# Attention output leaves PSUM in one copy and one addition per head, and is rounded and split once per pair

## The chip, the cores and the metric

The kernel runs on one core of a Trainium2 chip. The metric is the device time of one execution in microseconds (us). The matrix engine is TensorE (PE in the profile, PEld for its weight loads), the elementwise engines are VectorE (DVE), ScalarE (ACT) and GpSimd (POOL), and SyncE (SP) issues nearly all of the transfers (DMA). Matrix products are accumulated in PSUM, a memory of 128 partitions with banks of 512 float32 columns. All other data on the core lie in SBUF.

## The reference

Attention over 8 batches of 8 heads, 576 tokens, head size 64, with a decay and a causal mask; then a gated MLP over the 8 heads side by side (512 columns):

```python
scores = scale * np.matmul(q, k.transpose(0, 1, 3, 2))
cum = np.cumsum(np.log(np.clip(f, 0.0001, 1.0)), axis=-1)
scores = np.where(causal, -1000000000.0, scores + cum[:, :, :, None] - cum[:, :, None, :])
attn = np.exp(scores - np.max(scores, axis=-1, keepdims=True))
attn = attn / (np.sum(attn, axis=-1, keepdims=True) + 1e-09)
x = np.matmul(attn, v)                       # then heads side by side: [batch, 576, 512]
h = np.maximum(x @ w_in, 0.0)
u, v = h[..., :512], h[..., 512:]
v_n = (v - mean(v)) / np.sqrt(var(v) + 1e-06)
v_s = np.einsum('ts,bsd->btd', w_spatial, v_n) + b_spatial[None, :, None]
out = (u * v_s) @ w_out
```

## The kernel before

Heads are worked in 32 pairs, four pairs to a batch; a pair's first head lies on partitions 0 to 63, its second on 64 to 127. A float32 operand of a product is held as two parts, `hi` (x rounded to the type float32r) and `lo` (x - hi), and a product is the sum of hi*hi, hi*lo and lo*hi. In the first NF = 5 pairs the product of attention and values is done in plain float32 instead, with one weight operand; the first NQ = 1 pair also has plain float32 scores.

`attention` works one pair P at a time. It loads the values (`prep_v`: tile `vraw`, split into `vt` from pair 5 on), builds the score operands `ta` and `tb` of pair P + 1 by copies within SBUF (`prep`), transposes the attention of pair P (`transposes`, into `ET`), computes the scores of pair P + 1 (`scores`, `scores_tail`), loads and splits queries and keys of pair P + 2 (`split`: tile `raw`, rounded on ScalarE, line 210, subtracted on GpSimd, line 212), and multiplies by the values (`attend`, once for each head). `raw`, `vraw` and `vt` have one buffer each, so a load of the next `raw` waits until line 212 has read the last one, and a load of the next `vraw` until line 243 has (in the first five pairs: until the products have).

`attend` accumulates a head's 576 columns in two PSUM banks, `x0` (tokens 0 to 255) and `x1` (256 to 575). In the split pairs the weights are 128 columns wide, so that one half of the output partitions holds the products with the head's v_hi and the other half those with v_lo; the sum of the two halves is the result. For each bank, ScalarE rounds the first half into `xh` (line 373), VectorE subtracts it from the bank into `xl` (line 374), and, in the split pairs, VectorE adds the other half of the partitions to `xl` (line 376). After the pair's second head VectorE copies the last 64 columns of `xl` behind those of `xh` (line 416). `xh` and `xl` have five buffers: four are held by the batch that the MLP reads, and one by the pair in progress; they are taken before the first head's `attend`.

`moe` is the MLP of a batch. It reads `xh` and `xl` of four pairs in its first two stages, 5 and 8 accumulations with all four pairs in each, and then gives the four buffers back. Then come the spatial product and the output product.

The order in which instructions are issued is made by a planner at build time: it gets the instructions in the order in which the two generators `attention` and `moe` yield (attention runs ahead of the MLP by LEAD = 0.25 of a batch), and places each on its engine's queue by its own estimate of when operands and buffers are ready. On the chip each queue is then worked strictly in the planned order, SP's transfers too. A load of weights (`load64`, `load_rest`) in steps on VectorE, ScalarE and GpSimd runs beside the first pairs. The MLP can't begin a batch before its fourth pair is complete.

Of the kernel before, what the change touches and what calls it, by code (L numbers as in the profile page):

```python
# [8 lines left out]
F32 = mybir.dt.float32  # L9
# [10 lines left out]
NF = 5            # pairs of heads whose attention times v is in float32  # L20
NQ = 1            # pairs of heads whose scores are in float32
# [3 lines left out]
NB = 4            # full 128-token blocks; the last 64 tokens are the tail  # L25
TL = 512          # first token of the tail
DM = 512
TOFF = (0, 128, 384, 768)      # start of a block's scores in a head's score tile
HALVES = ((0, 256), (256, 320))      # (start, length) of the halves of the tokens
QK = 640 + S        # columns of a head's queries, then of its keys  # L30
EOFF = (0, 640, 1280, 1088, 576)   # start of a key chunk in a head's packed attention^T


def f32(ap):
    return ap.bitcast(F32)
# [3 lines left out]
def attn_gmlp_kernel(ctx: ExitStack, tc: tile.TileContext, qk, v, f, w_in, w_sp, b_sp, w_out, out):  # L39
    """Decayed causal attention, then a gated MLP with a spatial gate.  # L40

    A float32 operand x of a matrix product is held as two float32r parts, hi = x rounded to
    float32r and lo = x - hi, and a product is hi*hi + hi*lo + lo*hi, summed in float32.
    """
# [15 lines left out]
    ident = cst.tile([128, 128], F32, name="ident")  # L60
    make_identity(nc, ident)
    # [zeros 512 | causal 128 | zeros 224 | causal 64, for two stacked heads]
# [12 lines left out]
    # ---- decay rows of the score products: [-8 | c_hi], [-8 | c_lo], [c_hi | 8], [c_lo | 8],  # L75
    # the queries' columns as in qk, then the keys'; c = cumulated log decay; [-8 | c], [c | 8] in float32 ----
# [58 lines left out]
    def load64(src, dh, dl, raw, w, a, mark=None):  # L135
        """A block of a float64 weight, read as two 32-bit words: round to float32 and split."""
# [3 lines left out]
        # magnitude, at least 2**-127, so that what float32 can't hold becomes zero  # L140
        A.activation(af, hi.bitcast(F32), AF.Abs)
        V.tensor_scalar(out=af, in0=af, scalar1=2.0 ** -15, scalar2=None, op0=ALU.max)
        # sign, exponent and the upper 20 bits of the mantissa
        V.tensor_scalar(out=a, in0=a, scalar1=3, scalar2=0x3FFFFFF8, op0=ALU.logical_shift_left, op1=ALU.bitwise_and)
        V.scalar_tensor_tensor(out=w, in0=hi, scalar=0xC0000000, in1=a, op0=ALU.bitwise_and, op1=ALU.bitwise_or)
        # the lower 32 bits of the mantissa
# [6 lines left out]
    def load_first(ws):  # L153
        """What the first steps of the MLP need: w_in for the gate's half, the spatial weights."""
# [26 lines left out]
    def load_rest(n, w_v, dh, dl, tag, bufs):  # L181
        """An eighth of a weight, by way of tiles that the MLP doesn't use yet."""
        raw = mo.tile([128, NJ, 64, 2], U32, name="w64", tag=("gt0", "gt1", "o")[n % 3], bufs=1)
        w = mo.tile([128, NJ, 64], U32, name="w32", tag=tag, bufs=bufs)
        t = mo.tile([128, NJ, 64], U32, name="wa", tag=tag, bufs=bufs)
        c = slice(64 * n, 64 * n + 64)
        load64(w_v[:, :, c, :], dh[:, :, c], dl[:, :, c], raw, w[:], t[:])

# [13 lines left out]
    def split(P):  # L202
        """q and k of a pair of heads, one head on each half of the partitions, split."""
# [11 lines left out]
    def prep(P, h):  # L215
        """The operands of a head's scores: ta = [q_hi; q_lo | k_hi; k_hi], tb = [q_hi; decay | k_lo; decay]."""
# [29 lines left out]
    def qkt(o, P, h, q0, k0, n, first, final):  # L246
        """Scores of 128 queries against n keys."""
        k0 += 640
        ts = tab[P, h]
        for t in ts:  # L250
            r = 66 if len(ts) == 1 else 128 if t is ts[0] else 68
            mm(o, t[0:r, q0:q0 + 128], t[0:r, k0:k0 + n], first and t is ts[0], final and t is ts[-1])

    def scores(P, h):
        """Masked scores of a head, negated and scaled; row maxima; exp; row sums; normalised."""
# [94 lines left out]
    def attend(P, h, xh, xl):  # L350
        vt = vts[P]
        x0 = ps_a.tile([128, 512], F32, name="x0")
        x1 = ps_a.tile([128, 512], F32, name="x1")
# [16 lines left out]
        for ps, s0, n in ((x0, 0, 256), (x1, 256, 320)):  # L370
            hi = xh[m0:m0 + 64, s0:s0 + n]
            lo = xl[m0:m0 + 64, s0:s0 + n]
            last[P, h] = A.copy(hi, ps[m0:m0 + 64, 0:n])  # L373
            V.tensor_tensor(out=lo, in0=ps[m0:m0 + 64, 0:n], in1=f32(hi), op=ALU.subtract)  # L374
            if P >= NF:
                V.tensor_tensor(out=lo, in0=ps[l0:l0 + 64, 0:n], in1=f32(lo), op=ALU.add)
# [4 lines left out]
    def attention(b, ws=None):  # L381
        for P in range(b * PPB, (b + 1) * PPB):
            if P == 0:
# [3 lines left out]
                # products of zeros bring the tensor engine to its full clock before the first scores  # L387
                warm = ps_a.tile([128, 512], F32, name="x0")
                for _ in range(14):
                    mm(warm, zm[:, 0:128], zm[:, 0:512], True, True)  # L390
# [18 lines left out]
            xh = wk.tile([128, 640], F32R, name="xh", tag="xh", bufs=5)  # L409
            xl = wk.tile([128, S], F32R, name="xl", tag="xl", bufs=5)  # L410
            yield from attend(P, 0, xh, xl)
# [3 lines left out]
            yield from attend(P, 1, xh, xl)  # L415
# [7 lines left out]
    def acc(b):  # L423
        """A bank to accumulate in; the last batch has those of the attention too."""
# [193 lines left out]
```

## Time and profile before

| What | Value |
|---|---|
| Timed runs | 836.0, 832.36, 834.18 us; median 834.18 |
| Profiled execution, first to last instruction (span) | 827.5 us |
| Mean granted TensorE clock | 0.972 |
| TensorE busy | 791.4 us (96%) |
| VectorE busy | 608.6 us (74%) |
| ScalarE busy | 535.9 us (65%) |
| GpSimd busy | 464.7 us (56%) |
| Lines 373 / 374 / 376 / 416 | 49.6 / 57.4 / 48.8 / 16.8 us |

The profile has no time of the profiled execution other than its span; the timed runs contain what lies before and after it. Busy shares are averages over a start, in which weights are loaded and the first batch has no MLP beside it, a long middle, and an end without attention; the stretches are looked at one by one. Times within the span are counted from its first instruction.

### The profile page before, as it was taken

What the parts mean: (1) busy time and instruction counts of PE and PEld (TensorE: products, weight loads), DVE (VectorE), ACT (ScalarE), POOL (GpSimd) and SP (SyncE); (2) the same over time, 40 slices, a digit from 0 to 9 for tenths busy, and PEclk for the clock granted to TensorE, in tenths of its full rate; (3) what the DMA queues carried; (4) which work ended last, traced back from release to release, by engine and by line L of the source; (5) the groups of instructions that cost most, each with busy time, mean ns of one, the idle gap of its engine ahead of it and who ended that gap; (6) DMA issues with size and microseconds to landing.
All of it is one profiled execution on the core that took longest, in us unless ns stands there. A gap on an engine that the chain in (4) does not pass through costs nothing.

```text
span 827.5 us, 15557 instructions
## 1 busy us (share of the span) xinstructions
PE 791.4 (96%) x4968; PEld 711.3 (86%) x4968; DVE 608.6 (74%) x1830; ACT 535.9 (65%) x1383; POOL 464.7 (56%) x631
## 2 busy tenths in 40 slices
PE   7889898999999999999999999999999999999997
PEld 4667687879889998999899988898899988999896
DVE  5776998987788777787677776768776777776431
ACT  5888556765777657767677666666676657665331
POOL 5674788664585555555575555465664547543131
PEclk7799987999999999999999999999999999999999
DMA  8997747446653664556455564546535664430001
GB/s 234 209 260 194 192 134 183 106 109 164 165 137 96 141 170 118 128 111 165 129 129 139 139 137 117 130 105 157 150 78 124 165 154 117 109 77 13 27 1 64
DMA packets 49851, 109.16 MB, mean 132 GB/s; under 512 B 7405, under 2 KB 15597, under 8 KB 49706
## 3 DMA queue, kind: packets, MB, share of 16 engines
q1 hardware_dynamic: 49450, 107.64, 52.2%
q8 instruction: 40, 0.66, 0.3%
q10 hardware_dynamic: 320, 0.52, 0.2%
q14 instruction: 41, 0.34, 0.1%
HBM read 39.53 MB, written 10.68 MB: 61 GB/s over the span
## 4 chain that ended last, share of the span: by engine, by line
PE 71%; DVE 4%; DMA 1%; ACT 1%; POOL 1%; issue 1%; SPq 0%; ACTq 0%; POOLq 0%; DVEq 0%
PE ps L198 40%; PE sc L198 12%; PE x L198 9%; PE tp L325 6%; PE tp L198 2%; PE tp L338 2%; DMA out_dram<-o 1%; DVE vx L461 1%; DVE el L315 1%; POOL tt L277 1%; DVE xh L416 0%; ACT eh L314 0%; ACT o L534 0%; POOL mv L460 0%; DVE tt L264 0%
## 5 line engine op out<-in xcount | busy, mean ns | idle before, releaser
L277 POOL TENSOR_SCALAR tt<-tt,sm 128x128 f32<-128x128 f32 (+2 forms) x248 | 131.5, 548 | 110.8 <-DVE sm L270 91.0
L264 DVE CUSTOM_DVE_ANT_0 tt<-sc,zm 128x128 f32<-128x128 f32 (+3 forms) x256 | 122.5, 486 | 69.0 <-PE tp L325 44.5
L266 ACT ACTIVATE tt<-tt,nm 128x128 f32<-128x128 f32 (+3 forms) x256 | 144.1, 564 | 41.0 <-DVE nm L264 37.1
L314 ACT CAST eh<-tp 128x512 fp32r<-128x512 f32 (+1 forms) x270 | 110.8, 424 | 58.8 <-PE tp L325 42.0
L315 DVE TENSOR_TENSOR el<-tp,eh 128x512 fp32r<-128x512 f32 (+1 forms) x270 | 127.2, 484 | 14.7 <-ACT eh L314 11.1
L198 PE MATMUL sc<-ta 128*128 128x128 f32 (+1 forms) x372 | 122.8, 340 | 13.6 <-DVE nm L264 9.0
L198 PE MATMUL sc<-tb 68*128 68x128 f32 (+1 forms) x372 | 117.9, 325 | 2.2 <-DMA tb<-lo 1.7
L325 PE MATMUL tp<-ident,tt 128*128 128x128 f32 x640 | 115.4, 284 | 2.0 <-DVE el L315 1.1
L212 POOL TENSOR_TENSOR lo<-raw,hi 128x640 fp32r<-128x640 f32 (+1 forms) x62 | 92.3, 1509 | 21.1 <-ACT hi L210 20.9
L198 PE MATMUL x<-eh,vt 128*128 128x320 f32 (+4 forms) x378 | 102.5, 287 | 1.3 <-DVE eh L347 0.9
L510 POOL TENSOR_TENSOR gl<-u,gh 128x256 fp32r<-128x256 f32 (+1 forms) x64 | 51.8, 810 | 84.9 <-ACT gh L509 79.0
L198 PEld LDWEIGHTS sc<-ta 128*128 128x128 f32 x372 | 72.3, 196 | 22.3 <-DVE nm L264 15.9
L198 PE MATMUL x<-el,vt 128*128 128x256 f32 x324 | 91.2, 307 | 0.3 <-DVE el L315 0.3
L325 PEld LDWEIGHTS tp<-ident,tt 128*128 128x128 f32 x640 | 78.7, 143 | 13.5 <-POOL tt L277 2.6
L198 PEld LDWEIGHTS sc<-tb 68*128 68x128 f32 x372 | 72.3, 196 | 5.7 <-issue 2.7
L198 PE MATMUL ps<-sph,vnh 128*128 128x256 f32 (+1 forms) x240 | 73.4, 306 | 2.7 <-DVE u L506 1.6
L198 PEld LDWEIGHTS x<-eh,vt 128*128 128x128 f32 x378 | 71.4, 190 | 5.0 <-DVE eh L347 1.1
L198 PE MATMUL ps<-xh,winh 128*128 128x256 f32 (+1 forms) x232 | 71.1, 307 | 0.8 <-ACT u L484 0.6
L198 PE MATMUL ps<-sph,vnl 128*128 128x256 f32 (+1 forms) x240 | 71.6, 298 | 0.0
L198 PE MATMUL ps<-spl,vnh 128*128 128x256 f32 (+1 forms) x240 | 71.6, 298 | 0.0
L374 DVE TENSOR_TENSOR xl<-x,xh 64x256 fp32r<-64x256 f32 (+1 forms) x128 | 57.4, 452 | 18.5 <-ACT xh L373 16.1
L373 ACT CAST xh<-x 64x256 fp32r<-64x256 f32 (+1 forms) x128 | 49.6, 393 | 32.2 <-PE x L198 30.3
(192 smaller groups left out, 2128.9 us busy)
## 6 DMA issues: line engine op xcount, KB each, us to landing
raw<-in_dram SPq DMA_DIRECT2D x31, 608.0 KB
ta<-hi SPq DMA_DIRECT2D x62, 304.0 KB
vraw<-in_dram SPq DMA_DIRECT2D x32, 320.0 KB
tb<-hi SPq DMA_DIRECT2D x62, 160.0 KB
ta<-lo SPq DMA_DIRECT2D x62, 160.0 KB
tb<-lo SPq DMA_DIRECT2D x62, 144.0 KB
ta<-hi SPq DMA_DIRECT2D x62, 144.0 KB
out_dram<-o SPq DMA_DIRECT2D x32, 256.0 KB
```

Of the source, the lines that this page charges most:

```text
L198: T.matmul(o, l, r, start=st, stop=sp)
L212: G.tensor_tensor(out=lo[:, c], in0=raw[:, c], in1=f32(hi[:, c]), op=ALU.subtract)
L264: V.tensor_tensor_reduce(out=t, in0=sc[:, 0:n], in1=zm[:, 640 - n:640], scale=-0.125, scalar=3.0e38, op0=ALU.add, op1=ALU.min, accum_out=n ...
L266: last["exp", P, h, i] = A.activation(t, t, AF.Exp, bias=nm[:, i:i + 1], scale=-1.0, accum_out=sm[:, i:i + 1])
L277: G.tensor_scalar(out=t, in0=t, scalar1=sm[:, i:i + 1], scalar2=1.0, op0=ALU.mult, op1=ALU.mult)
L314: A.copy(h_ap, ps)
L315: V.tensor_tensor(out=l_ap, in0=ps, in1=f32(h_ap), op=ALU.subtract)
L325: T.transpose(out=tp[:, (i - c) * 128:(i - c + 1) * 128], in_=tt[h][:, TOFF[i] + 128 * c:TOFF[i] + 128 * c + 128], identity=ident)
L338: T.transpose(out=tp[:, j * 128:(j + 1) * 128], in_=tl[:, c * 128:(c + 1) * 128], identity=ident)
L373: last[P, h] = A.copy(hi, ps[m0:m0 + 64, 0:n])
L374: V.tensor_tensor(out=lo, in0=ps[m0:m0 + 64, 0:n], in1=f32(hi), op=ALU.subtract)
L510: G.tensor_tensor(out=gl[j][:, 0:nt], in0=g, in1=f32(gh[j][:, 0:nt]), op=ALU.subtract)
```

## The change

A head's 576 columns now lie side by side in one tile of two banks, `xp`: x0 is its columns 256 to 511 and x1 its columns 512 to 831, so that they are one row of 576 columns that crosses from the first bank to the second. ScalarE copies the row out in float32 in one instruction into a new tile `xf`; in the split pairs it copies the half with the v_lo products, and VectorE adds the other half in one instruction. After both heads, the whole pair (128 partitions) is rounded in one ScalarE instruction and subtracted on GpSimd in two (64 and 512 columns). `xh` and `xl` are taken only then. `xf` has no memory of its own: it takes its turn in the one buffer of `raw` (pairs 0 to 4) or of `vraw` (from pair 5). The rest of the diff removes comments.

```diff
-    def attend(P, h, xh, xl):
+    def attend(P, h, xf):
         vt = vts[P]
-        x0 = ps_a.tile([128, 512], F32, name="x0")
-        x1 = ps_a.tile([128, 512], F32, name="x1")
+        xp = ps_a.tile([128, 1024], F32, name="xp")
+        x0, x1 = xp[:, 256:512], xp[:, 512:832]
...
         m0, l0 = (0, 64) if h == 0 else (64, 0)
-        for ps, s0, n in ((x0, 0, 256), (x1, 256, 320)):
-            hi = xh[m0:m0 + 64, s0:s0 + n]
-            lo = xl[m0:m0 + 64, s0:s0 + n]
-            last[P, h] = A.copy(hi, ps[m0:m0 + 64, 0:n])
-            V.tensor_tensor(out=lo, in0=ps[m0:m0 + 64, 0:n], in1=f32(hi), op=ALU.subtract)
-            if P >= NF:
-                V.tensor_tensor(out=lo, in0=ps[l0:l0 + 64, 0:n], in1=f32(lo), op=ALU.add)
+        o = xf[m0:m0 + 64, :]
+        if P >= NF:
+            A.copy(o, xp[l0:l0 + 64, 256:832])
+            last[P, h] = V.tensor_tensor(out=o, in0=xp[m0:m0 + 64, 256:832], in1=o, op=ALU.add)
+        else:
+            last[P, h] = A.copy(o, xp[m0:m0 + 64, 256:832])
...
-            xh = wk.tile([128, 640], F32R, name="xh", tag="xh", bufs=5)
-            xl = wk.tile([128, S], F32R, name="xl", tag="xl", bufs=5)
-            yield from attend(P, 0, xh, xl)
+            xf = wk.tile([128, S], F32, name="xf", tag="raw" if P < NF else "vraw")
+            yield from attend(P, 0, xf)
             yield from transposes(P, 1)
             if nxt:
                 yield from scores(P + 1, 1)
-            yield from attend(P, 1, xh, xl)
+            yield from attend(P, 1, xf)
+            xh = wk.tile([128, 640], F32R, name="xh", tag="xh", bufs=5)
+            xl = wk.tile([128, S], F32R, name="xl", tag="xl", bufs=5)
+            A.copy(xh[:, 0:S], xf)
+            for t in (slice(TL, S), slice(0, TL)):
+                G.tensor_tensor(out=xl[:, t], in0=xf[:, t], in1=f32(xh[:, t]), op=ALU.subtract)
             V.tensor_copy(xh[:, S:640], f32(xl[:, TL:S]))
```

More of the change, by code (lines that the diff above doesn't have):

```diff
@@ L386, in attention @@
                     prep(0, h)
-                warm = ps_a.tile([128, 512], F32, name="x0")
+                warm = ps_a.tile([128, 1024], F32, name="xp")
                 for _ in range(14):
-                    mm(warm, zm[:, 0:128], zm[:, 0:512], True, True)
+                    mm(warm[:, 0:512], zm[:, 0:128], zm[:, 0:512], True, True)
                 split_rows(ws, r0s[0])
```

## Prediction

> **What bounds the kernel now.** I read the engine totals first, then stretches of the span, then who TensorE waits for.
>
> ```profile
> PE 791.4 (96%) x4968; PEld 711.3 (86%) x4968; DVE 608.6 (74%) x1830; ACT 535.9 (65%) x1383; POOL 464.7 (56%) x631
> ```
>
> The stretches (columns: PE, PEld, DVE, ACT, POOL busy us, granted clock, DMA share):
>
> ```profile
> 60.00:100.00 40.00, 37.48 (x194) 29.02 (x192) 29.52 (x97) 31.52 (x83) 24.15 (x31) 0.98 0.78 199
> 100.00:180.00 80.00, 70.07 (x402) 61.32 (x403) 76.03 (x206) 48.86 (x134) 57.95 (x78) 0.87 0.55 139
> 500.00:600.00 100.00, 96.59 (x629) 89.05 (x628) 75.92 (x232) 66.30 (x172) 56.99 (x81) 1.00 0.52 128
> ```
>
> From 200 us on TensorE is the bound: even in this stretch, the one of that part with the most idle time, it is busy for 96.6 of 100 us, at the full granted clock. Only from 100 to 180 us is another engine fuller: VectorE 76.0 of 80 us, while TensorE idles 10 us and its clock falls to 0.87. What TensorE waits for, from 100 to 200 us:
>
> ```profile
> PE sc L198 <- DVE nm L264: 6.7, 7, 1.9
> ```
>
> and from 200 to 800 us:
>
> ```profile
> PE ps L198 <- DVE u L506: 2.6, 4, 1.1
> PE sc L198 <- DVE nm L264: 2.1, 3, 1.2
> ```
>
> The longest waits of TensorE are on VectorE in both parts, but they are small: about 7 us early and 5 us in the 600 us after. The change leaves every matrix product as it is, so a lighter VectorE can give back these waits, at most the 10 us of idle time of the full stretch, and no more.
>
> **The instructions.** Groups by line and shape (busy us, mean ns):
>
> ```profile
> L373 ACT CAST xh<-x 64x320 fp32r<-64x320 f32 x64 | 26.8, 419 | 23.8 <-PE x L198 23.1
> L373 ACT CAST xh<-x 64x256 fp32r<-64x256 f32 x64 | 23.5, 366 | 8.4 <-PE x L198 7.2
> L374 DVE TENSOR_TENSOR xl<-x,xh 64x320 fp32r<-64x320 f32 x64 | 31.0, 485 | 8.8 <-ACT xh L373 7.7
> L374 DVE TENSOR_TENSOR xl<-x,xh 64x256 fp32r<-64x256 f32 x64 | 26.8, 418 | 9.7 <-ACT xh L373 8.4
> L376 DVE TENSOR_TENSOR xl<-x,xl 64x320 fp32r<-64x320 f32 x54 | 26.3, 488 | 1.6
> L376 DVE TENSOR_TENSOR xl<-x,xl 64x256 fp32r<-64x256 f32 x54 | 22.8, 422 | 1.7
> L164 ACT CAST sph<-wraw 128x576 fp32r<-128x576 f32 x4 | 2.6, 664 | 0.0
> L465 POOL TENSOR_TENSOR vnl<-vx,vnh 128x512 fp32r<-128x512 f32 x32 | 41.5, 1306 | 15.6 <-ACT vnh L463 15.4
> L297 POOL TENSOR_SCALAR tl<-tl,sm 128x64 f32<-128x64 f32 x27 | 8.7, 323 | 27.7 <-DVE sm L295 9.2 <-ACT vx L456 4.8 <-PE sc L198 4.4
> ```
>
> No row reads 576 columns across two banks. 64 more columns cost VectorE 66 ns (488 - 422) and ScalarE 53 ns (419 - 366), so an addition over 576 is 488 + 4 x 66 = 752 ns and a copy 419 + 4 x 53 = 631 ns. If the bank crossing cost as much as a second instruction they would be 910 and 785 ns (the present pairs); I take the lower, since one instruction pays its fixed part once.
> - VectorE: off go 31.0 + 26.8 + 26.3 + 22.8 = 106.9 us, on come 54 x 0.752 = 40.6 us (27 pairs in split precision, two heads): **-66 us**. With 910 ns it is -58.
> - ScalarE: off 50.3, on 64 x 0.631 + 32 x 0.664 = 61.6: **+11 us**, 65% to 66% of the span; no bound anywhere.
> - GpSimd: 32 x (1.306 + 0.323) = **+52 us**, 56% to 62%.
>
> The Trainium skill ("Advanced Engine Details and Errata", The Read-Write Bubble) says that the memory latency shows between instructions, so larger tiles are better, and that one instruction may read several PSUM banks. The 66 ns per 64 columns beside 422 ns for 256 agree; by that rule the 752 ns stands.
>
> GpSimd work is not free for VectorE:
>
> ```profile
> L416 DVE CAST xh<-xl x32: 175/324/1590, 49.6 to 780.7; 128x64 fp32r<-128x64 f32 x32
> L374 DVE TENSOR_TENSOR xl<-x,xh x128: 381/446/495, 30.3 to 779.0; 64x256 fp32r<-64x256 f32 x64, 64x320 fp32r<-64x320 f32 x64
> ```
>
> L416, from SBUF to SBUF, stretches from 175 ns to 1590; L374, which takes one operand from PSUM, stays within 381 to 495. The new addition is of the second kind. The three or so pairs evacuated between 100 and 180 us add 3 x 1.63 = 4.9 us to GpSimd's 58; at worst VectorE waits all of it, at best none. I take 1.5.
>
> The Trainium skill ("SBUF — State Buffer", Who interferes with whom) calls this an exclusive lock on a port pair that VectorE and GpSimd share. If each new subtraction blocked VectorE for its whole length, the early gain below would shrink from 4.4 to 1 us.
>
> **Early gain.** What goes in the full stretch, 100 to 180 us:
>
> ```profile
> L374 DVE TENSOR_TENSOR xl<-x,xh 64x320 fp32r<-64x320 f32 (+1 forms) x12 | 5.3, 449 | 0.2
> L376 DVE TENSOR_TENSOR xl<-x,xl 64x256 fp32r<-64x256 f32 (+1 forms) x7 | 3.2, 451 | 0.2
> ```
>
> VectorE loses 5.3 + 3.2 = 8.5 us there and would do some 3.5 additions (2.6 us): 5.9 less, 1.5 lost to GpSimd: **-4.4 us** where VectorE is the bound. After 200 us a tenth less VectorE work takes some 1.5 of the 5 us of waits: **-1.5**.
>
> **The borrowed buffers.** The new tile xf sits in the one buffer of `raw` (pairs 0 to 4) or of `vraw` (from pair 5). Both are loaded ahead today; now the next load must wait for the last subtraction of the pair, and SP's later loads queue behind it. Start, pair 4's load and split and pair 1's last products and evacuation (pairs counted by the order of their loads and copies):
>
> ```profile
> 55.76 0.36 SPq L207 DMA_DIRECT2D raw<-in_dram  x1
> 61.11 2.56 PE L198 MATMUL x<-ef,vraw 128*128 128x320 f32 x10
> 61.34 1.21 ACT L210 CAST hi<-raw 128x1216 fp32r<-128x1216 f32 x1 [0.23 <-DMA wraw<-in_dram]
> 63.89 2.93 POOL L212 TENSOR_TENSOR lo<-raw,hi 128x640 fp32r<-128x640 f32 x2
> 64.93 0.42 ACT L373 CAST xh<-x 64x320 fp32r<-64x320 f32 x1
> 69.11 0.49 DVE L374 TENSOR_TENSOR xl<-x,xh 64x320 fp32r<-64x320 f32 x1
> 101.69 0.49 DVE L374 TENSOR_TENSOR xl<-x,xh 64x320 fp32r<-64x320 f32 x1
> ```
>
> `raw` of pair 4 goes out at 55.8 but pair 1 is finished at 69.6: the load comes 14 us later, and pair 2's evacuation must in turn wait for pair 4's split, 66.8 - 55.8 = 11 us after its load. A turn of this loop is 11 + copy 0.6 + the second head's 14 products 3.5 (ten of them took 2.56, four 0.92 further down) + copy 0.6 + cast 0.7 + subtractions 1.6 + some 2.2 of queueing (as measured further down) = 20.2 us, against 69.6 to 102.2 = 16.3 per pair now (the last row is pair 3's). From pair 1 to pair 3 that makes the first batch 2 x 3.9 = 8 us late, and with it the start of the MLP. VectorE is idle for 10.5 us between 60 and 100 us, which the weight loads can fill meanwhile, so I charge less than half: **+3.5** (0 to 8).
>
> Later, from the end of pair 17's products to the start of pair 18's, and a `vraw` load that TensorE waited for:
>
> ```profile
> 63.70 0.34 SPq L237 DMA_DIRECT2D vraw<-in_dram  x1
> 66.71 0.92 PE L198 MATMUL x<-ef,vraw 128*128 128x256 f32 x4 [0.43 <-DMA vraw<-in_dram]
> 418.30 0.42 ACT L373 CAST xh<-x 64x320 fp32r<-64x320 f32 x1
> 442.33 0.68 ACT L373 CAST xh<-x 64x256 fp32r<-64x256 f32 x2
> 448.70 0.21 PE L198 MATMUL x<-eh,vt 128*128 128x64 f32 x1
> 449.56 0.73 ACT L242 CAST vt<-vraw 128x640 fp32r<-128x640 f32 x1
> 450.37 1.56 POOL L243 TENSOR_TENSOR vt<-vraw,vt 128x640 fp32r<-128x640 f32 x1 [1.41 <-ACT vt L242]
> 451.95 0.36 SPq L237 DMA_DIRECT2D vraw<-in_dram  x1
> 452.03 0.49 DVE L376 TENSOR_TENSOR xl<-x,xl 64x320 fp32r<-64x320 f32 x1
> 453.75 0.37 PE L198 MATMUL x<-eh,vt 128*128 128x256 f32 x1
> ```
>
> Now it is 448.9 to 453.75 = 4.9 us. Today's evacuation ends 452.5 - 448.9 = 3.6 us after the products, 1.4 of it the three instructions on the last 320 columns, so 2.2 is queueing. After the change: copy 0.63, addition 0.75, cast 0.66, subtractions 1.63, the same 2.2, load 3.0 (63.70 to 66.71), L242 0.73, L243 1.56, 1 more of queueing = 12.2 us: 7.3 later per pair. What hides it: TensorE has the MLP's products to run, and attention idles 24 us at a batch boundary (418.30 to 442.33), waiting for an xh buffer. That wait softens too, since products now land in xf without one. Three exposed turns cost 22 of these 24 us, so I charge only **+0.8** for TensorE orders that miss by a little. If the cover is gone it is the third rival below.
>
> What is queued behind that load on SP:
>
> ```profile
> SPq L237 <- POOL vt L243: 92.8, 23, 6.3
> 458.61 0.47 SPq L227 DMA_DIRECT2D ta<-hi  x1
> ```
>
> SP already stands at this load for 4 us in 23 pairs (92.8 / 23), waiting for vt's subtraction. With the change the load of 451.95 would go out at 448.9 + 5.9 = 454.8, still ahead of the next `ta` load at 458.61, which the scores of the pair after next need. So the queue is not stretched here; a `vraw` load that is 4 us later than I reckon would begin to hold the score operands back too.
>
> **Smaller steps.** The rounded pair is complete 5.9 us after its products instead of 3.6. The MLP reads it with a pair in hand, so these 2.3 us show only for the last pair, where TensorE has other accumulations open: 0, at most 2. The two banks are now one buffer, so the next head's products wait for copy and addition, 1.38 us, as long as the last three instructions did (1.4): 0.
>
> Sum on the profiled span: 827.5 - 4.4 - 1.5 + 3.5 + 0.8 = 825.9. The median of the timed runs, 834.18, is 6.7 above the span; with it **832.6 us**.
>
> **Rivals.**
> - *The lighter VectorE pays in full*: the 10 us that TensorE idles in the full stretch go, 3 of the 5 us of later waits too, and the late loads cost 2: 834.2 - 13 + 2 = 823. For it: VectorE's 76 of 80 us. Against: GpSimd is at 58 of those 80, and gets more.
> - *The raw loop decides at the start*: slower. From the point where its turn exceeds 16 us, the first batch ends 8 us late; unabsorbed, less 2 of gain: 840. For it: 11 us from load to split. Against: VectorE's idle time before 100 us.
> - *The vraw loop decides throughout*: slower. Three turns at 12.2 + 2.2 (queues twice as long) - 4.9 = 9.5 make 28.5 against 24 us of cover: 4.5 x 6.75 batches = 30; half of it refilled by MLP products, 849. Against: SP waits at this very load today (above), and TensorE does not feel it.
>
> **Chances.** No change 0.37, full pay 0.36, raw loop 0.16, vraw loop 0.11. A difference under 0.5% (4.2 us) can't be told from none here. The likeliest is the sum, 832.6, with 829 to 838 as its own range; the range 818 to 849 takes in the 823 less 5 (additions that free more waits than TensorE's own rows show) and the vraw loop. Faster 0.36, same 0.37, slower 0.27.
>
> **What would show it.** VectorE near 543 us, GpSimd near 516, additions near 752 ns. Right: VectorE under 72 of 80 us from 100 to 180 us, TensorE waits on VectorE there below 5 us, and no TensorE wait on vt. Wrong: `raw` loads that follow the subtractions at once with TensorE idle before 120 us, or waits of the x products for vt or its load in the steady part. A TensorE busy under 96 of 100 us after 200 us would overturn the forecast.

## The result and the profile after

The changed kernel takes 865.68 us in the median of 4 runs (863.68 to 869.62), the kernel before 834.22 beside it: a ratio of 1.0386 (95% interval 1.0349 to 1.0423). It is slower by 3.9%; 832.6 had been predicted, with 849 as the upper end of the range. The span of the profiled execution grows from 827.5 to 867.8 us; the changed kernel's profiled execution is the slowest of its four runs (869.62 us), so the 40.3 us between the spans are more than the 31.5 us between the medians.

The totals by engine (busy us, share of the span, instructions), and the stretches (columns as in the prediction: PE, PEld, DVE, ACT, POOL, granted clock, DMA share, GB/s), of the kernel after:

```profile
PE 804.0 (93%) x4968; PEld 713.6 (82%) x4968; DVE 573.1 (66%) x1648; ACT 540.7 (62%) x1351; POOL 513.9 (59%) x695
```

```profile
60.00:100.00 40.00, 27.29 (x119) 21.02 (x120) 23.76 (x68) 22.22 (x57) 20.63 (x26) 0.80 0.71 181
100.00:180.00 80.00, 70.88 (x406) 60.03 (x405) 67.38 (x190) 51.81 (x134) 63.35 (x84) 0.94 0.62 156
200.00:300.00 100.00, 92.77 (x609) 85.58 (x608) 64.37 (x191) 61.29 (x156) 57.56 (x81) 0.98 0.53 126
400.00:500.00 100.00, 94.93 (x613) 87.31 (x612) 64.81 (x192) 61.64 (x157) 56.88 (x79) 0.97 0.51 126
```

VectorE did get lighter, from 608.6 to 573.1 us, and between 100 and 180 us from 76.0 to 67.4. But no engine is fuller than TensorE in any of these stretches, and TensorE itself has lost: 27.3 instead of 37.5 us between 60 and 100 us, and it is idle for 7.2 and 5.1 us in the two later stretches, where the kernel before was idle for 1.2 and 0.3 us:

```profile
200.00:300.00 100.00, 98.75 (x659) 91.58 (x658) 80.08 (x243) 70.07 (x183) 58.36 (x81) 1.00 0.57 136
400.00:500.00 100.00, 99.73 (x658) 91.85 (x657) 72.91 (x231) 66.84 (x175) 55.66 (x78) 1.00 0.57 140
```

Most of the 40.3 us is work that comes late: TensorE's idle time grows from 36.1 to 63.8 us, by 27.7. The other 12.6 us are busy time, 804.0 instead of 791.4 us for the same 4968 instructions. The mean granted clock of the profiled execution is 0.965 instead of 0.972, and in the two later stretches it is 0.98 and 0.97 instead of 1.00; whether the idle time brings the lower clock with it is not separated by any run here. The groups of the changed lines (out<-in shapes xcount | busy us, mean ns | idle before, and what ended it):

```profile
L419 POOL TENSOR_TENSOR xl<-xf,xh 128x512 fp32r<-128x512 f32 x32 | 41.2, 1287 | 0.0
L374 DVE TENSOR_TENSOR xf<-xp,xf 64x576 f32<-64x576 f32 x54 | 40.6, 752 | 12.5 <-ACT xf L373 11.6
L373 ACT COPY xf<-xp 64x576 f32<-64x576 f32 x54 | 34.3, 634 | 54.7 <-PE xp L198 54.1
L420 DVE CAST xh<-xl 128x64 fp32r<-128x64 f32 x32 | 30.8, 963 | 3.4 <-POOL xl L419 3.1
L417 ACT CAST xh<-xf 128x576 fp32r<-128x576 f32 x32 | 21.6, 676 | 1.9 <-DVE xf L374 1.8
L419 POOL TENSOR_TENSOR xl<-xf,xh 128x64 fp32r<-128x64 f32 x32 | 10.6, 330 | 31.0 <-ACT xh L417 31.0
```

The two-bank addition and the copy take what was worked out. L420, the same cast as L416 before, went from 524 to 963 ns in the mean.

**The start.** One turn of the buffer of `raw`, from one pair's subtraction to the next pair's (timeline: start us, duration us; L376 here is the copy of the unsplit pairs):

```profile
54.24 1.55 POOL L419 TENSOR_TENSOR xl<-xf,xh 128x64 fp32r<-128x64 f32 x2
55.82 0.33 SPq L207 DMA_DIRECT2D raw<-in_dram  x1
...
60.89 2.89 POOL L212 TENSOR_TENSOR lo<-raw,hi 128x640 fp32r<-128x640 f32 x2
63.82 0.63 ACT L376 COPY xf<-xp 64x576 f32<-64x576 f32 x1 [3.01 <-POOL lo L212]
...
75.39 1.57 POOL L419 TENSOR_TENSOR xl<-xf,xh 128x64 fp32r<-128x64 f32 x2 [11.61 <-ACT xh L417]
77.16 0.33 SPq L207 DMA_DIRECT2D raw<-in_dram  x1
...
99.97 0.33 SPq L207 DMA_DIRECT2D raw<-in_dram  x1
...
124.87 0.34 SPq L207 DMA_DIRECT2D raw<-in_dram  x1
```

Each `raw` load goes out as the subtraction ends (54.24 + 1.55 = 55.79, then 55.82), and each first copy of `xf` starts as `raw` has been split (60.89 + 2.89 = 63.78, then 63.82). The turns are 21.3, 22.8 and 24.9 us, 23.0 in the mean. TensorE feels it as waits for the score operands, which are made from `raw` (waits of TensorE, 0 to 200 us: total us, times, longest us):

```profile
PE tp L325 <- DVE ef L310: 9.9, 7, 3.5
PE sc L198 <- DMA ta<-lo: 8.4, 3, 4.3
```

**The steady part.** One turn of the buffer of `vraw` (pair 21 of 0 to 31):

```profile
553.74 0.36 SPq L237 DMA_DIRECT2D vraw<-in_dram  x1
557.00 0.72 ACT L242 CAST vt<-vraw 128x640 fp32r<-128x640 f32 x1
560.24 1.57 POOL L243 TENSOR_TENSOR vt<-vraw,vt 128x640 fp32r<-128x640 f32 x1
...
573.44 0.63 ACT L373 COPY xf<-xp 64x576 f32<-64x576 f32 x1
574.12 0.76 DVE L374 TENSOR_TENSOR xf<-xp,xf 64x576 f32<-64x576 f32 x1
576.07 0.68 ACT L417 CAST xh<-xf 128x576 fp32r<-128x576 f32 x1
579.17 1.57 POOL L419 TENSOR_TENSOR xl<-xf,xh 128x64 fp32r<-128x64 f32 x2
580.77 0.36 SPq L237 DMA_DIRECT2D vraw<-in_dram  x1
```

The load leaves 30 ns after the last subtraction (580.74). ScalarE now waits for the load itself, which it practically never did before (instructions of L242: median duration, first and last start, and what ended the idle time before them; first the kernel before, then the one after):

```profile
L242 ACT CAST vt<-vraw x27: 725/727/729, 131.0 to 756.5; 128x640 fp32r<-128x640 f32 x27
...
  DMA vraw<-in_dram: 1.0, 1
```

```profile
L242 ACT CAST vt<-vraw x27: 713/727/731, 146.7 to 795.8; 128x640 fp32r<-128x640 f32 x27
its engine sat idle before it (us, times) until:
  DMA vraw<-in_dram: 46.6, 23
```

The first L242 starts 15.7 us later than before, the last one 39.3, and the span is 40.3 longer. So the loss in this profile is the lateness of attention: about 16 us by the end of the first five pairs and about 24 over the 27 after them. In the chain of waits that ended last, the longest pieces are this load (start us, us):

```profile
201.54 6.17 DMA vraw<-in_dram
255.74 7.40 DMA vraw<-in_dram
```

### The profile page after: what moved, and what is told of

Its sections match the earlier page's. It is cut to its first block, busy times and chain, and to the rows that moved or that the text cites. A ratio compares the mean times of both kernels' runs of the same rounds, so it can differ in the third digit from the quotient of the medians.

```text
span 867.8 us, 15398 instructions
## 1 busy us (share of the span) xinstructions
PE 804.0 (93%) x4968; PEld 713.6 (82%) x4968; DVE 573.1 (66%) x1648; ACT 540.7 (62%) x1351; POOL 513.9 (59%) x695
## 4 chain that ended last, share of the span: by engine, by line
PE 51%; DMA 11%; DVE 8%; ACT 7%; POOL 6%; issue 3%; SPq 2%; ACTq 0%; POOLq 0%; DVEq 0%
PE ps L198 28%; PE xp L198 8%; PE sc L198 8%; DMA vraw<-in_dram 7%; PE tp L325 4%; POOL lo L212 3%; DMA out_dram<-o 2%; PE tp L198 1%; ACT eh L314 1%; DVE vx L465 1%; ACT tt L266 1%; DVE el L315 1%; POOL tt L277 1%; DMA tb<-lo 1%; ACT hi L210 1%
## 5 line engine op out<-in xcount | busy, mean ns | idle before, releaser
L198 PE MATMUL sc<-ta 128*128 128x128 f32 (+1 forms) x372 | 120.9, 338 | 17.1 <-DMA ta<-lo 8.4
L325 PE MATMUL tp<-ident,tt 128*128 128x128 f32 x640 | 110.9, 284 | 17.2 <-DVE ef L310 9.9
L198 PE MATMUL xp<-eh,vt 128*128 128x320 f32 (+4 forms) x378 | 86.8, 284 | 0.9 <-DVE xf L374 0.9
L198 PE MATMUL xp<-el,vt 128*128 128x256 f32 x324 | 74.2, 296 | 0.0
L198 PEld LDWEIGHTS xp<-eh,vt 128*128 128x128 f32 x378 | 67.5, 191 | 2.4 <-DVE xf L374 1.1
L198 PE MATMUL ps<-xh,winl 128*128 128x256 f32 (+1 forms) x232 | 69.3, 299 | 0.0
L198 PE MATMUL ps<-winh,xh 128*128 128x512 f32 x148 | 62.6, 423 | 7.1 <-ACT vx L460 6.0
```

What stands on the lines that cost most here:

```text
L198: T.matmul(o, l, r, start=st, stop=sp)
L325: T.transpose(out=tp[:, (i - c) * 128:(i - c + 1) * 128], in_=tt[h][:, TOFF[i] + 128 * c:TOFF[i] + 128 * c + 128], identity=ident)
```

## The experiments

Each time stands beside runs of the kernel before on the same chip; their medians lie between 830.6 and 833.5 us. Kernels in which `xf` has a buffer of its own have the launch's scratch cut from 2048 to 1024, since that buffer doesn't fit otherwise. The ratios and intervals are those on record and not quotients of the medians beside them; with few runs the two differ by up to 0.3 points (own buffer: 1.0122, while 843.18 / 830.64 is 1.0151), so a difference of 3 us between two kernels is in doubt.

**1. The buffers of xf.** Its own buffer throughout; `raw`'s in pairs 0 to 4 and its own after; its own first and `vraw`'s after:

```diff
-            xf = wk.tile([128, S], F32, name="xf", tag="raw" if P < NF else "vraw")
+            xf = wk.tile([128, S], F32, name="xf", tag="xf")                          # e1
+            xf = wk.tile([128, S], F32, name="xf", tag="raw" if P < NF else "xf")     # e2
+            xf = wk.tile([128, S], F32, name="xf", tag="xf" if P < NF else "vraw")    # e3
```

> The changed kernel, but xf has a buffer of its own for all pairs (the scratch that the launch sets aside is cut from 2048 to 1024 to make room). Theory 1 (the borrowed buffers turn the attention into a chain of one load after another, 25.0 us per pair from pair 5 to 31 instead of 23.5): loads go ahead again, 822 to 838 us. Theory 2 (the new evacuation itself is slow: 50 us more GpSimd work, which blocks VectorE, and a pair complete later): it stays at 855 to 868 us.

> xf borrows the buffer of raw in pairs 0 to 4, and has its own from pair 5 on. Theory 1: the start stays 16 us late at pair 5, the rest runs at 23.5 us per pair; part of the delay is caught up, 838 to 852 us. Theory 2: 855 to 868 us.

> xf has its own buffer in pairs 0 to 4 and borrows that of vraw from pair 5 on. Theory 1: the start is as early as before the change, then 25.0 us per pair: 834 + 26 x 1.5 = 850 to 868 us if the later loop decides alone. If the start decides, 834 to 842 us. Theory 2: 855 to 868 us.

Measured: own buffer 843.18 us, ratio 1.0122 (1.0083 to 1.0161); `raw` only 847.71, 1.0183 (1.0146 to 1.0220); `vraw` only 849.40, 1.0210 (1.0178 to 1.0242). 843.18 lies between the ranges of the two theories, 847.71 in that of theory 1, and 849.40 just below theory 1's 850. So the borrowed buffers cost 22.5 us (865.7 - 843.2; 22.0 by the ratios), but one at a time 4.5 and 6.2 (5.1 and 7.3 by the ratios): together 10 to 12 us more than their sum. And 1.2% stay without any borrowing, which the prediction had not seen at all.

That the two work on each other shows first in the `vraw` loads. The load of pair 5, and then the first and the last of all 32 (the last number before the semicolon), first with `raw` alone borrowed, then with `vraw` alone:

```profile
142.61 0.52 SPq L237 DMA_DIRECT2D vraw<-in_dram  x1
...
L237 SPq DMA_DIRECT2D vraw<-in_dram x32: 328/352/516, 3.3 to 736.3; - x32
```

```profile
124.39 0.35 SPq L237 DMA_DIRECT2D vraw<-in_dram  x1
...
L237 SPq DMA_DIRECT2D vraw<-in_dram x32: 328/491/1508, 3.3 to 772.6; - x32
```

and with both:

```profile
142.85 0.49 SPq L237 DMA_DIRECT2D vraw<-in_dram  x1
...
L237 SPq DMA_DIRECT2D vraw<-in_dram x32: 327/460/1423, 3.3 to 793.0; - x32
```

In the kernel before these two loads stand at 126.89 and 736.7. With `raw` alone the 16 us of delay are made up: pair 6's load follows after 6.5 us, and the last load is where it was. With both, pair 5 is 18.5 us later than with `vraw` alone, and the last pair is still 20.4 us later.

Why the delay of the start is made up in one case and kept in the other shows in a wait that serves as a reserve. In the changed kernel a pair takes its `xh` buffer only when it is rounded, and the second pair of each batch (5, 9, 13, ...) has to wait there until the MLP has read, for the last time, the `xh` of the first pair of the batch before. Pair 5 in the kernel with its own buffer, the last product that reads pair 0's `xh`, and then the rounding, whose idle time ahead the profile puts down to a product (`PE ps`):

```profile
174.44 0.47 PE L198 MATMUL ps<-xh,winl 128*128 128x320 f32 x1
...
174.95 0.67 ACT L417 CAST xh<-xf 128x576 fp32r<-128x576 f32 x1 [0.16 <-PE ps L198]
```

The time from the end of a pair's addition to its rounding, in these pairs (us, worked out from the starts and ends of L374 and L417; in the pairs between them it is at most 3.4):

```
pair           5     9    13    17    21    25    29
own buffer  20.8   8.3  12.8   5.8  11.6   3.6  12.1
raw only     4.0   8.5  12.8   5.8  11.6   3.6  12.1
vraw only   14.3  10.6   8.9   2.0   0.2   1.5   0.3
both         3.4   1.5   0.0   0.2   1.2   1.2   0.2
```

While a pair waits like this, attention is ahead, and a delay shortens the wait. With `raw` alone the late start is paid out of the first wait, and all later ones are as they were. With `vraw` alone the longer turns have used the waits up by pair 17. With both 3.4 us are left at pair 5 and nothing after it. TensorE's lateness follows: measured against the kernel before at the same amount of products done (each counted with its median spacing in the trace before), it is 4.6 us at 200 us, 7.4 at 500 and 18.9 at 700 with `vraw` alone, and 11.6, 32.8 and 38.8 us with both.

**2. The turn, with more work in it, and without the rest of the change.** The kernel after with the 512-column subtraction issued twice (the second writes the same values again); then the kernel before with an unread tile dm that takes a turn in `vraw`'s buffer from pair 5 on (e4), and the same tile in its own buffer (e8):

```diff
-            for t in (slice(TL, S), slice(0, TL)):
+            for t in (slice(TL, S), slice(0, TL), slice(0, TL)):
```

```diff
             yield from attend(P, 1, xh, xl)
+            if P >= NF:
+                dm = wk.tile([128, S], F32, name="dm", tag="vraw")      # e4; e8: tag="dm"
+                A.copy(dm, f32(xl[:]))
+                G.tensor_tensor(out=dm, in0=dm, in1=f32(xh[:, 0:S]), op=ALU.subtract)
```

> The changed kernel with the subtraction over 512 columns issued twice (the same values twice), 1.29 us more on GpSimd per pair, between a pair's evacuation and the next load. Theory 1: every turn is 1.3 us longer, 26 turns + 4 at the start: 895 to 908 us. Rival (the turn has slack, and only some fixed stalls cost): 862 to 872 us.

> The kernel before, with its own evacuation; from pair 5 on a tile of 576 columns takes a turn in the buffer of vraw after each pair: ScalarE copies xl into it and GpSimd subtracts xh from it (128 x 576 each, the work that the change adds per pair); nothing reads the result. Theory 1: the next vraw load waits for it as in the changed kernel, so 850 to 870 us. Theory 2, in the form that one copy and one addition over two banks are slow: this kernel has neither and stays at 832 to 842 us.

> The kernel before with the same added copy and subtraction per pair as in the run that gave 853.96 us, but their tile in a buffer of its own, so that no load waits for it. Theory 1: the wait was the cost, 832 to 840 us. Rival: the added work was the cost, 850 to 857 us.

Measured: doubled 866.16 us, 1.0401 (1.0375 to 1.0427), no longer than the kernel after; e4 853.96, 1.0270 (1.0230 to 1.0309); e8 849.92, 1.0195 (1.0155 to 1.0235). The doubled subtraction refutes a loop in which every instruction counts with its full length. The mean parts of a turn show where its 1.3 us went (pairs 7 to 30, us, from the starts and ends of the rows named; e17 belongs to experiment 5):

```
                                       after   doubled   e17
load out to end of L243                 7.48     6.21    6.26
to the first product                    1.87     2.11    2.19
to the first head's copy                2.15     2.56    2.44
to the second head's copy               6.05     5.14    8.05
to the end of its addition              1.64     1.73    1.60
to the pair's rounding                  1.33     0.35    1.46
to the end of the last subtraction      3.75     5.84    2.30
to the next load                        0.37     0.27    0.08
turn                                   24.64    24.20   24.36
```

The subtractions end 2.1 us later, but the load, L242 and L243 take 1.3 us less and the rounding starts 1.0 us earlier; the likely reason, not tested, is that the planner, which knows of the longer subtraction, put other work elsewhere. There was queueing to be taken out. The dummy kernels say less than they were meant to: most of the cost of e4 is there without any turn in `vraw`'s buffer (e8), by the added 18 us on ScalarE and 39 on GpSimd. From e8 to e4, the turn itself, it is 4 us (6 by the ratios; the two intervals just meet).

**3. Is it the order?** Any edit makes the planner write another order. Three kernels shift the order of the kernel before and leave its work alone (13 or 15 products of zeros at the start instead of 14; the second bank taken out first), and one that of the kernel after:

```diff
-                for _ in range(14):
+                for _ in range(13):            # e9; e10: 15
```

```diff
-        for ps, s0, n in ((x0, 0, 256), (x1, 256, 320)):
+        for ps, s0, n in ((x1, 256, 320), (x0, 0, 256)):      # e11, the kernel before
...
-            for t in (slice(TL, S), slice(0, TL)):
+            for t in (slice(0, TL), slice(TL, S)):            # e12, the kernel after
```

> The kernel before with 13 instead of 14 products of zeros at the start (0.3 us of TensorE less). No operation that the change touches is touched, but the order written out for the engines comes out another one for nearly all of it. Theory A (the order of the kernel before is by chance a good one, and whatever shifts it costs about 1 to 2%): 838 to 850 us. Theory B (the 1.2% of the own-buffer kernel and the 1.5% of the kernel with the wide copies alone are the price of what these kernels do): 830 to 836 us, within 0.5% of the kernel before.

> The kernel before with 15 instead of 14 products of zeros at the start, another order again. Theory A: 838 to 850 us. Theory B: 830 to 836 us. One of the two such kernels within 0.5% and the other 1% above would say that orders differ by chance by this much and that the kernel before is not alone among the good ones.

> The kernel before with the two parts of a pair taken out of PSUM in the other order, the 320 columns of the second bank first. The same instructions with the same durations. Theory A (a shifted order costs 1 to 2%): 838 to 850 us. Theory B (durations and buffers decide): 830 to 837 us.

> The kernel after with the subtraction over 512 columns ahead of the one over 64. The same instructions and the same buffers, another order for the engines. Theory A, in its strongest form (all 3.9% is the order): the time moves by more than 1%, to anywhere in 835 to 880 us. Rival (the two buffer turns are in the way whatever the order, 2.5 to 3% above the own-buffer kernel): 859 to 872 us, and the vraw load again follows the last subtraction at once.

Measured: 830.99 us, 0.9984 (0.9962 to 1.0006); 832.04, 1.0005 (0.9978 to 1.0032); 831.23, 0.9978 (0.9959 to 0.9997); and for the kernel after 859.07, 1.0311 (1.0271 to 1.0351). Theory A falls: three other orders of the kernel before are all as fast, so it isn't a lucky one among these, and 1 to 2% in a variant are not explained by a shifted order alone. The kernel after is more sensitive: the same work in another order gave 0.8% back, less than theory A asked for, and 859.07 is at the edge of the rival's range. Single differences of that size between kernels with a borrowed buffer are therefore not read below.

**4. The evacuation: two banks as one tile, or wide instructions?** The kernel before with one 576-column copy, subtraction and addition per head and no `xf` (e5); the kernel before with the two banks in one tile and its narrow instructions kept (e13); and, against the cut scratch, the kernel before with a scratch of 1024 (e16):

```diff
-        x0 = ps_a.tile([128, 512], F32, name="x0")
-        x1 = ps_a.tile([128, 512], F32, name="x1")
+        xp = ps_a.tile([128, 1024], F32, name="xp")           # e5, e13
+        x0, x1 = xp[:, 256:512], xp[:, 512:832]
...
-        for ps, s0, n in ((x0, 0, 256), (x1, 256, 320)):
+        for ps, s0, n in ((xp[:, 256:832], 0, S),):           # e5 alone
```

> The kernel before with one part of the change alone: x0 and x1 in one tile, and lines 373, 374 and 376 once each over 576 columns instead of twice; rounding, subtraction and addition stay where they were, and xh and xl are written straight from PSUM. Theory 1 (what is left at xf's own buffer, 1.2%, comes from the subtraction on a full GpSimd in the start): 826 to 834 us. Theory 2 (it comes from the evacuation over two banks, which can't start at x0 before x1 is done and holds both banks): 837 to 846 us.

> The kernel before, its copies and subtractions of 256 and 320 columns left as they are, but both banks in one tile xp. Theory C (what costs is that the first 256 columns can no longer be taken out while the products of the other 320 still accumulate): if the buffer is handed over as a whole, the first copy no longer starts 3.8 us ahead of a head's last product but behind it, and the time is 838 to 848 us; if the copies still start ahead of it, 830 to 836. Theory D (the single long instructions of 634 and 752 ns hold up the short ones queued behind them): 830 to 836 us either way.

> The kernel before with the launch's scratch cut from 2048 to 1024, as all kernels with an own buffer for xf have it. If the scratch costs nothing: 830 to 836 us. If it is what costs the own-buffer kernel its 1.2%: 839 to 846 us.

Measured: e5 845.60 us, 1.0151 (1.0123 to 1.0179); e13 841.37, 1.0110 (1.0073 to 1.0147); e16 833.00, 1.0018 (0.9996 to 1.0039). The scratch is not the cause. One tile costs 1.1% with every instruction as it was. Groups of L373 in e13:

```profile
L373 ACT CAST xh<-xp 64x320 fp32r<-64x320 f32 x64 | 26.9, 420 | 7.1 <-DVE xl L376 5.7 <-DVE xl L374 0.6
...
L373 ACT CAST xh<-xp 64x256 fp32r<-64x256 f32 x64 | 23.4, 366 | 36.0 <-PE xp L198 34.9 <-PE tp L325 0.6
```

The durations are those of the kernel before (419 and 366 ns). What has changed is the idle time ahead: the copy of the first 256 columns waits 34.9 us for products, before it was 7.2, and the copy of the 320 columns no longer waits for products at all (23.1 before). A head's products in the kernel before, and the copy of its first bank in the middle of them:

```profile
548.54 0.27 PE L198 MATMUL x<-el,vt 128*128 128x128 f32 x1
548.85 0.36 ACT L373 CAST xh<-x 64x256 fp32r<-64x256 f32 x1 [0.77 <-PE x L198]
550.58 0.31 PE L198 MATMUL x<-eh,vt 128*128 128x320 f32 x1
...
552.15 0.28 PE L198 MATMUL x<-eh,vt 128*128 128x64 f32 x1
```

The first bank is finished at 548.8 and leaves while TensorE, with other products between, works on the second for another 3.6 us. Over the heads of pairs 5 to 31 the median copy starts 3.8 us ahead of the head's last product in the kernel before, 0.3 us behind it in e13, 0.04 behind it in e5; in e13 the last instruction on the banks ends 5.8 us after the last product, before it was 2.6. So the tile is handed over as a whole, after its last product, and theory D falls: the long instructions are not needed for the loss. Whether the wide instructions cost anything on top (1.51 against 1.10%) the intervals don't settle. They gain nothing: VectorE has 17 us less to do in e5 than before (591.4 against 608.6).

**5. Two tiles again, and the subtraction on VectorE.** The change with its own buffer and two tiles, each with its own copy and addition (e14); the subtraction in one 576-column instruction on VectorE instead, with the wide (e6) and with the narrow evacuation (e15); and both edits in the borrowed buffers (e17 on VectorE, e18 with two tiles):

```diff
-            A.copy(o, xp[l0:l0 + 64, 256:832])                                    # e14, e15, e18
-            last[P, h] = V.tensor_tensor(out=o, in0=xp[m0:m0 + 64, 256:832], in1=o, op=ALU.add)
+            for ps, s0, n in ((x0, 0, 256), (x1, 256, 320)):
+                on = o[:, s0:s0 + n]
+                A.copy(on, ps[l0:l0 + 64, 0:n])
+                last[P, h] = V.tensor_tensor(out=on, in0=ps[m0:m0 + 64, 0:n], in1=on, op=ALU.add)
...
-            for t in (slice(TL, S), slice(0, TL)):                                # e6, e15, e17
-                G.tensor_tensor(out=xl[:, t], in0=xf[:, t], in1=f32(xh[:, t]), op=ALU.subtract)
+            V.tensor_tensor(out=xl[:], in0=xf, in1=f32(xh[:, 0:S]), op=ALU.subtract)
```

> The changed kernel with xf in its own buffer (as in the first run) and the subtraction of a pair on VectorE in one instruction instead of on GpSimd in two. Theory 1: GpSimd is as free as before the change, 826 to 835 us. Theory 2: 838 to 845 us as with xf's own buffer.

> The change with its own buffer for xf (scratch of the launch cut to 1024, as in the own-buffer kernel), but with x0 and x1 as two tiles again, each taken out by its own copy and addition; rounding and subtraction once a pair stay. Theory C: the first copy is ahead of a head's last product again and the time falls from 843 to 828 to 835 us. Rival E (the 52 us of work on GpSimd and the longer path to xl cost the 1.2%, not the copies): 839 to 846 us.

> As the kernel with narrow copies and its own buffer, but the pair's subtraction in one instruction on VectorE. Theory C: 824 to 833 us, since VectorE still does less than before and GpSimd no more. Rival E (the path to xl): 836 to 843 us, like the same kernel with the wide copies (836.5).

> The kernel after, xf in the borrowed buffers, with the pair's subtraction in one instruction on VectorE instead of two on GpSimd. The time from the pair's rounding to the last subtraction (3.75 us in the mean of pairs 7 to 30 in the kernel after, for 1.6 us of work) should fall to 1 to 2 us. Theory F (the turn through the borrowed buffers is what costs, so a turn shorter by 2 us gives more than the 0.75% that the same exchange gave with an own buffer): 840 to 856 us. Rival (costs add up; only the 0.75% are got back): 857 to 863 us.

> The kernel after, xf in the borrowed buffers and the subtractions on GpSimd, with x0 and x1 as two tiles and a copy and an addition for each. If costs add up (own buffer: two tiles instead of one gave 0.5%): 859 to 863 us. If the borrowed buffers leave no room for an early first copy (products come late and at once there): 864 to 869 us. Much less than 855 would say that the 2.7% of the borrowed buffers holds only with the one tile.

Measured (us, ratio and interval to the kernel before):

```
                     subtraction on GpSimd               subtraction on VectorE
own, one tile        e1   843.18  1.0122 (1.0083-1.0161)  e6   836.51  1.0046 (1.0022-1.0070)
own, two tiles       e14  837.88  1.0071 (1.0048-1.0094)  e15  831.51  1.0002 (0.9976-1.0028)
borrowed, one tile   after 865.68 1.0386 (1.0349-1.0423)  e17  850.63  1.0198 (1.0165-1.0231)
borrowed, two tiles  e18  862.75  1.0350 (1.0311-1.0389)
```

The times of e6 and e14 lie between the ranges of their theories. With an own buffer the parts add up: one tile costs 0.4 to 0.5%, the subtraction on GpSimd 0.7 to 0.8% over the same on VectorE, and without both the kernel is as fast as before, within 0.3%. Theory C holds in its direction; it had expected e14 to get back all of the 1.2% and e14 got back 0.5, so that rival E, the GpSimd work, has the larger part of it. That part is there early: at the same amount of products done as in the kernel before at 200 us, e14 is 4.9 us behind e15, and e1 10.8 behind e6; between the ends of the spans it is 8.2 and 6.3. What GpSimd's work does to VectorE shows in the cast of the last 64 columns, first with the subtraction on GpSimd (e14), then on VectorE (e15):

```profile
L422 DVE CAST xh<-xl 128x64 fp32r<-128x64 f32 x32 | 26.0, 814 | 2.6 <-POOL xl L421 2.5
```

```profile
L421 DVE CAST xh<-xl 128x64 fp32r<-128x64 f32 x32 | 16.7, 523 | 0.2
```

In the borrowed buffers the same exchange is worth 15.1 us (865.7 - 850.6) instead of 6.4 to 6.7, as theory F expected: there the subtraction stands in both turns. Its group in e17:

```profile
L418 DVE TENSOR_TENSOR xl<-xf,xh 128x576 fp32r<-128x576 f32 x32 | 39.8, 1245 | 7.2 <-ACT xh L417 6.8
```

By the table of turns the path from rounding to the last subtraction is 2.30 us instead of 3.75, and load and split take 1.2 us less too. But the second head's copy comes 2.0 us later, so that a turn of `vraw`'s buffer is only 0.3 us shorter (24.36 against 24.64), some 7 us over 25 turns. More is gained in the start: the three turns of `raw`'s buffer take 21.0 us in the mean instead of 23.0, and at 200 us of the kernel before TensorE is 0.1 us late instead of 11.6, which is more than half of the 19.0 us between the two spans. From 200 to 300 us it is busy for 98.6 of 100 us again:

```profile
200.00:300.00 100.00, 98.60 (x652) 90.77 (x651) 73.13 (x216) 67.52 (x171) 57.35 (x77) 1.00 0.51 127
```

In e18 two tiles give 2.9 us, inside the range for costs that add up; a difference of this size is not read further here.

No variant of the change beats the kernel before. The best, e15, has the change's arithmetic without its buffers, its one tile and its engine, and is equal to it.

## Why the prediction was wrong

Right were the instructions: the addition 752 ns (forecast 752), the copy 634 (631), the rounding 676 (664), the subtractions 1287 and 330 (1306 and 323), and with them GpSimd at 513.9 us (516). VectorE was to fall to 543 us and fell to 573.1: the removed and added lines come out as reckoned, but other instructions got longer, 30.8 us in all, the cast of L420 alone 14 us (16.8 to 30.8). The rule of the Trainium skill ("Advanced Engine Details and Errata", The Read-Write Bubble) that one instruction may read several PSUM banks agrees: 752 ns for 576 columns across two banks, against 422 + 488 in two instructions. It is of no use here. What failed is where time was worth something.

- **Early gain, -4.4 and -1.5: not seen.** Between 100 and 180 us VectorE did fall to 67.4 of 80 us, as forecast, and TensorE's waits on line 264 fell from 6.7 to 2.6 us. But TensorE's busy time there rose by 0.8 us only (70.07 to 70.88), as other waits took their place. "VectorE 76 of 80 us" was read as a bound that hands back whatever is taken off it. In e15 VectorE has 18 us less to do in all (590.4) for 0.02% of time; in this stretch, though, it is still busy for 73.1 of 80 us, so a kernel that relieves it there and changes nothing else was not tried.
- **GpSimd's work, +1.5: +6.4 to 6.7 us** (e14 against e15, e1 against e6), the exchange of engines as a whole. It was priced as VectorE's waiting beside the three pairs between 100 and 180 us. Most of it is there by 200 us, and the price was too low; by which wait it reaches TensorE is not shown.
- **The raw loop, +3.5 (0 to 8): +4.5** (e2 against e1). Mechanism and size hold as long as the values are loaded ahead. The turn was reckoned at 20.2 us and took 23.0; pair 5 comes 16 us late, not 8; and 11 or 12 of the 16 us are paid by the wait of pair 5 (20.8 us in e1, 4.0 in e2) and not, as reckoned, by VectorE's idle time. That the sum came out near is in part luck.
- **The vraw loop, +0.8: +6.2 alone** (e3 against e1), and this is the step that failed most. From a pair's last products to the next pair's first it was reckoned at 12.2 us with 3.2 of queueing; by the table of turns it is 1.64 + 1.33 + 3.75 + 0.37 + 7.48 + 1.87 = 16.4 us, of which the same instructions and the load are again about 9. The queueing is 7.4 us. Three turns that are 16.4 - 4.9 = 11.5 us longer make 34.5, more than the 24 us of cover. And the cover itself was too large: the 24 us (418.30 to 442.33) lie between two copies of the kernel before, while the wait for an `xh` buffer, where there is one to use up, is 3.6 to 12.8 us a batch in e1 from pair 9 on. It was used up, not left.
- **The sum itself.** The two loops were added as if independent, but both are paid from the same waits. The first takes the one of pair 5, the second those of the later pairs, and with both nothing is left after pair 5: 10 to 12 us more than the two alone.
- **"The two banks are now one buffer ... 0": +4 to 5 us** in the own-buffer kernels (e1 against e14, e6 against e15), and 9 in e13, where the narrow instructions hold the tile for 5.8 us after the last product. The prediction compared what is left to do after the last product, 1.38 against 1.4 us, and overlooked that the first bank leaves 3.8 us ahead of it.

Of the rivals, the lighter VectorE that pays in full has nothing for it in these runs. The vraw loop had the mechanism and the side: its 849 is what it costs when it alone is borrowed (849.4), but that kernel holds the one tile and GpSimd's work too, so the agreement is not a confirmation of its 28.5 us against 24. The raw loop's 840 has its mechanism right. Of the signs named as contrary two are there: `raw` loads at once behind the subtractions with TensorE idle before 120 us, and TensorE under 96 of 100 us after 200 us. Waits of the `x` products for `vt` are not: the likely reason is that the planner has put other products ahead, and the longest wait of TensorE after 200 us is 6.0 us in all, for an MLP operand:

```profile
PE ps L198 <- ACT vx L460: 6.0, 3, 2.9
```

Added up from the runs: one tile and the work on GpSimd 1.2% (e1), `raw` 0.6%, `vraw` 0.9%, both together another 1.2%: 3.9%. What stays open: how the microseconds of the one tile reach TensorE. No single wait of TensorE holds them in e13. In its profiled execution TensorE is idle for 6.1 us more than in the kernel before (42.2 against 36.1) and busy for 9.1 more (800.5 against 791.4), at a mean granted clock of 0.958 instead of 0.972. The late copies are shown, their way through the planned order is only argued.

## What to carry to other kernels

Before a tile borrows the buffer of a load that runs ahead, ask how much waiting the pipeline has left that can pay for the delay: here the waits at the batch boundaries paid for one loop and not for two, so the price shows only beside another delay. Count a turn with the queueing that the trace shows on each engine in it. Two banks that are finished at different times are worth two tiles, even where one instruction could read both. An engine that is busy for 95% of a stretch is a bound only if the one that sets the end waits for it.

## What was not expected of the hardware

What stretches the 64-column cast on VectorE in the kernel after is mostly one neighbour, not GpSimd's total. In the kernel after it becomes ready when the subtraction over the same 64 columns ends, and that is when GpSimd begins the one over 512. Of its 32 instances 26 run beside that subtraction and take 1075 ns in the mean, the other six 480, and the one beside which GpSimd runs nothing 185. In e12, where the 512 columns come first, none runs beside it:

```profile
L420 DVE CAST xh<-xl 128x64 fp32r<-128x64 f32 x32 | 14.4, 451 | 5.7 <-POOL xl L419 5.5
```

That is 963 ns down to 451 with the same work on GpSimd; how much of the 6.6 us between the two kernels it is was not tried. The Trainium skill ("SBUF — State Buffer", Who interferes with whom) names a port pair that the two engines share under a lock; the row agrees.
